# Attention with adapters on one core: a static list scheduler sets the order of all engines

## The chip, the core and the metric

The kernel runs on one core of a Trainium2 chip. The core has a matrix engine (TensorE, PE), three other compute engines (VectorE or DVE, ScalarE or ACT, GpSimd or POOL) and a queue engine (SyncE, SP) that here only issues transfers. Each engine works through its own list of instructions in program order and waits at semaphores for the others; DMA transfers run beside them. The metric is the device time of one execution in microseconds (us).

## The reference

For 8 batches and 8 heads, with 576 positions of 64 values, it computes attention with a relative bias, and sends the result, 4608 rows of 512, through a mixture of 8 low-rank adapters of which each row takes the best two:

```python
scores = (1 / sqrt(64)) * q @ k.T + bias_table[bucket(|i - j|)]   # per head
x = softmax(scores) @ v                                            # then heads side by side
logits = x @ w_gate                                                # (4608, 8)
w = softmax over the two largest logits
out = x + sum over those two e of w[e] * (x @ A[e]) @ B[e]         # A (512,16), B (16,512)
```

The bias depends only on the distance and is constant from distance 128 on, so the kernel multiplies exp(scores) by exp(bias - last bias) in a band around the diagonal, and nowhere else.

## The kernel before

The work goes by pairs of heads: 4 pairs a batch, 32 pairs in all (i). The first 512 positions are the main part; the last 64 of all heads of a batch (the "tails") are loaded and transposed once per batch. For each pair SP loads k, q and v as f32, POOL casts them to bf16 (`cast_kq`, `cast_v`), PE transposes k and q into a PSUM tile kqps (`transposes`), and DVE copies that to kqT. Then come five steps (c = 0 to 4, the last one for the tails): PE makes scores into one of two PSUM tiles sc (`qk`), ACT takes their exp in one instruction of 128x1024 (`softmax_exp`), DVE multiplies the band in place (`band`). PE multiplies the probabilities by v, with a column of ones for the sums, into the only accumulator pv (`pv`, parts 0 to 5); DVE takes the reciprocal rc and writes x (`norm`).

After the fourth pair of a batch its adapters follow, as a list of small pieces (`pieces`): transposes of x (xps to xT), gate logits (lp, lg), the best two by DVE's maximum, df and mk, a small exp on ACT (ex), the gate weights, z (zp to zt), its transpose (zT), and four output tiles (dl to o) that SP stores. Every second batch also sends the tail rows of two batches through. All PSUM tiles but sc and pv share two buffers, "ms".

The order is written out by hand. The main loop goes over i and c; at each step it issues the scores of the next step, the exp of this one, the band of the last one, and the PV parts of the pair before in fixed slots. Loads for pair i + 4, casts for i + 2 and the tail loads of the next batch have slots too, and `BUD` gives each step a budget of adapter pieces, taken from a queue. At the start SP's queue holds k of pair 0 and the tails of batch 0, then the bias chain (the table goes through g_sb, an exp and DRAM, and comes back as the Toeplitz tiles Mr and MHr, from which DVE makes M, MT, MH and MHT), then pairs 1 to 3.

Of the kernel before, what the change touches and what calls it, by code (L numbers as in the profile page):

```python
# [10 lines left out]
FP32 = mybir.dt.float32  # L11
# [16 lines left out]
def kernel(  # L28
# [25 lines left out]
    ctx.enter_context(tc.manual_schedule())  # L54
    cp = ctx.enter_context(tc.tile_pool(name="const", bufs=1))
# [6 lines left out]
    op = ctx.enter_context(tc.tile_pool(name="outs", bufs=4))  # L62
# [16 lines left out]
    def load(i, e0=None, e1=None):
        b, hp = divmod(i, HP)  # L80
        kf = ldp.tile([128, 4, 2, D], FP32, name="kf", tag="kf")
        qf = ldp.tile([128, 2, 256], FP32, name="qf", tag="qf")
        load_nat(kf, k, i, e0 or SY)
        (e1 or SY).dma_start(out=qf, in_=q[b, 2 * hp:2 * hp + 2, 0:S4, :]
                             .rearrange("h (p j) d -> p h (j d)", j=4))
        stg[i] = [kf, qf, None]

    def load_v(i):
        b, hp = divmod(i, HP)
        vf = ldp.tile([128, 4, 2, D], FP32, name="vf", tag="vf")  # L90
        load_nat(vf, v, i, SY)
        stg[i][2] = vf

    def load_tails(b):
        tf = ldp.tile([128, H, D], FP32, name="tf", tag="tf", bufs=2)
        SY.dma_start(out=tf[0:64], in_=k[b, :, S4:, :].rearrange("h p d -> p h d"))
        SY.dma_start(out=tf[64:128], in_=q[b, :, S4:, :].rearrange("h p d -> p h d"))
        tstg[b] = [tf, None]

    def load_vtails(b):  # L100
        vtf = ldp.tile([128, HP, D], FP32, name="vtf", tag="vtf", bufs=2)
        vtr = v[b, :, S4:, :].rearrange("(c e) p d -> e p c d", e=2)
        for e in range(2):
            SY.dma_start(out=vtf[e * 64:(e + 1) * 64], in_=vtr[e])
        tstg[b][1] = vtf
# [28 lines left out]

    def cast_vtail(b, e=None):
        vt = vts[b % 2]
        for h in range(2):
            s = slice(h * 64, (h + 1) * 64)
            copy_on(e or PL, vt[s, :, h * D1:h * D1 + D], tstg[b][1][s])
        tstg.pop(b)  # L140

    load(0, SY, AC)
    load_tails(0)
    btT = cp.tile([H, NB], FP32, tag="btT")
    AC.dma_start(out=btT, in_=bias_table.rearrange("b h -> h b"))
    ident = cp.tile([128, 128], BF16, tag="ident")
    make_identity(nc, ident)

    cast_kq(0, DVE, AC)
    cast_tail(0, DVE)  # L150
    for t in tlTs:
        PL.memset(t, 0.0)
    for t in vts:
        PL.memset(t, 0.0)
        PL.memset(t[0:64, :, D:D1], 1.0)
        PL.memset(t[64:128, :, 2 * D + 1:2 * D1], 1.0)
    for t in vns:
        PL.memset(t[:, :, :, D:D1], 1.0)

    g_sb = cp.tile([H, 512], FP32, tag="g_sb")  # L160
    DVE.memset(g_sb, 0.0)
    bsub = cp.tile([H, NB], FP32, tag="bsub")
    DVE.tensor_scalar(bsub, btT, btT[:, NB - 1:NB], None, op0=ALU.subtract)
    buckets = [_bucket(d, NB) for d in range(256)]
    lo = 0
    runs = []
    for d in range(1, 129):
        if d == 128 or buckets[d] != buckets[lo]:
            runs.append((buckets[lo], lo, d))
            lo = d  # L170
    assert all(x == NB - 1 for x in buckets[128:])
    nsm = 0
    while runs[nsm][0] == nsm and runs[nsm][2] == nsm + 1:
        nsm += 1
    DVE.tensor_copy(g_sb[:, C:C + nsm], bsub[:, :nsm])
    DVE.tensor_copy(
        g_sb[:, C - nsm + 1:C],
        bass.AP(tensor=bsub.tensor, offset=bsub.offset + nsm - 1,
                ap=[bsub.ap[0], [-1, nsm - 1]]))
    for bv, lo, hi in runs[nsm:]:  # L180
        n = hi - lo
        dst = bass.AP(tensor=g_sb.tensor, offset=g_sb.offset + C - hi + 1,
                      ap=[g_sb.ap[0], [hi - 1 + lo, 2], [1, n]])
        DVE.tensor_copy(dst, bsub[:, bv:bv + 1].unsqueeze(2)
                        .to_broadcast((H, 2, n)))
# [11 lines left out]

    def load_bias(h0, h1):
        SY.dma_start(
            out=Mr[:, h0:h1, :],  # L200
            in_=bass.AP(tensor=gt.tensor, offset=gt.offset + h0 * 512,
                        ap=[[1, 128], [512, h1 - h0], [1, MW]]))

    load_bias(0, 2)
    for e in range(2):
        SY.dma_start(
            out=MHr[e * 64:(e + 1) * 64],
            in_=bass.AP(tensor=gt.tensor, offset=gt.offset + e * 512 + 192,
                        ap=[[1, 64], [1024, HP], [1, 192]]))

    def rev(t, o, w, dims):
        return bass.AP(tensor=t.tensor, offset=t[:, o, w:w + 1].offset,
                       ap=[t.ap[0]] + dims)

    def bias_pair(hp, e):
        e.tensor_copy(M[:, 2 * hp:2 * hp + 2],
                      rev(Mr, 2 * hp, 383, [[MW, 2], [-1, 4], [-4, 96]]))

    def bias_tail(e):
        e.tensor_copy(MT, rev(Mr, 0, 127, [[MW, H], [-1, 64]]))  # L220
        e.tensor_copy(MH, rev(MHr, 0, 191, [[192, HP], [-1, 4], [-4, 32]]))
        e.tensor_copy(MHT, rev(MHr, 0, 63, [[192, HP], [0, 2], [-1, 64]]))

    load(1)
    load_v(0)
    load_vtails(0)
    load_bias(2, H)
    load_v(1)
    load(2)
    load_v(2)  # L230
    load(3)
    load_v(3)

# [7 lines left out]

    def load_weights():
        for c in range(4):
            SY.dma_start(out=A_f[:, c], in_=moe_A[:, c * 128:(c + 1) * 128, :]
                         .rearrange("e d r -> d e r"))
        SY.dma_start(out=W_f, in_=moe_w_gate.rearrange("(c p) e -> p c e", p=128))
        SY.dma_start(out=B_f, in_=moe_B.rearrange("e r d -> (e r) d"))

    def cast_weights():
        PL.tensor_copy(Ab, A_f.rearrange("p c e r -> p c (e r)"))  # L250
        PL.tensor_copy(Wb, W_f)
        PL.tensor_copy(Bb, B_f)
        PL.memset(sel, 0.0)
        for e in range(2):
            for hf in range(2):
                s = slice(hf * 64, (hf + 1) * 64)
                PL.tensor_copy(sel[s, e, hf, e * 64:(e + 1) * 64], ident[s, s])


    def tails_T(b):  # L260
        tl = st.pop((b, "tl"))
        ps = msp.tile([128, HP, 2, 64], BF16, name="tps", tag="ms")
        for c in range(HP):
            nc.tensor.transpose(ps[:, c].rearrange("p w s -> p (w s)"),
                                tl[:, 2 * c:2 * c + 2, :], ident)
        t = tlTs[b % 2]
        for e in range(2):
            s = slice(e * 64, (e + 1) * 64)
            DVE.tensor_copy(t[s, :, 0:2, s], ps[s])
        DVE.tensor_copy(t[:, :, 2, :].rearrange("p c (w s) -> p c w s", w=2),  # L270
                        ps[:, :, 1:2, :].to_broadcast((128, HP, 2, 64)))
        tlT[b] = t

    def tails_sc(b):
        t = tlT[b]
        ps = msp.tile([128, HP, 128], FP32, name="ttps", tag="ms")
        for c in range(HP):
            nc.tensor.matmul(ps[:, c, :], lhsT=t[:, c, 0, :], rhs=t[:, c, 2, :],
                             start=(c == 0), stop=True, skip_group_check=True)
# [363 lines left out]
```

## Time and profile before

| | us |
|---|---|
| median of two timed runs | 273.56 (273.54 to 273.57) |
| the profiled execution | 271.94 |
| its span, first to last instruction | 270.1 |
| DVE busy | 210.2 |
| PE busy | 200.9 |
| ACT busy | 163.8 |
| POOL busy | 79.6 |

The mean clock granted to PE was 0.892 of full speed. Busy time is a sum over stages with different limits; what ends a wait is read from the views by stage. PE's matmuls are pipelined and their ends are modelled, so its busy time says more than its use.

### The profile page before, as it was taken

To read this page: it belongs to the slowest core of one execution; us is meant where nothing else is said; L and a number is where in the kernel's file an instruction comes from. 1 tells how busy PE (TensorE), PEld (TensorE's weight loads), DVE (VectorE), ACT (ScalarE), POOL (GpSimd) and SP (SyncE) were. 2 spreads that over 40 slices of the span, in tenths; PEclk is the share of its full clock that TensorE was granted. 3 is DMA by queue.
4 is the path that set the end of the run, shared out by engine and by line. 5 is a ranking of instruction groups with operands and counts; after the bars stand their busy time and mean duration, and the time that the engine had idled before them with its cause. 6 is when DMAs were issued, how large, how long until landed. Compare 5 with 4: busy or idle time off the path is not lost.

```text
span 270.1 us, 7307 instructions
## 1 busy us (share of the span) xinstructions
PE 200.9 (74%) x2872; PEld 139.5 (52%) x2872; DVE 210.2 (78%) x568; ACT 163.8 (61%) x183; POOL 79.6 (29%) x143
## 2 busy tenths in 40 slices
PE   0547918896798698868978598868886897868572
PEld 0224606575566565656556465646564665655540
DVE  1537745887797989896989879898988699869772
ACT  2445843955797568665686477756785677658000
POOL 7035268462211622126312411143315220000000
PEclk9999975997999899986999689988999599979955
DMA  4199998973239922885468803983498503102205
GB/s 117 39 244 238 160 236 224 249 188 79 86 115 242 212 74 93 244 211 139 147 173 198 207 4 113 270 206 97 159 244 204 120 34 137 29 2 77 83 0 194
DMA packets 101082, 39.76 MB, mean 147 GB/s; under 512 B 87088, under 2 KB 96312, under 8 KB 101048
## 3 DMA queue, kind: packets, MB, share of 16 engines
q1 hardware_dynamic: 100512, 39.03, 55.8%
q8 instruction: 22, 0.36, 0.6%
q10 hardware_dynamic: 536, 0.26, 0.4%
q14 instruction: 12, 0.10, 0.1%
HBM read 29.84 MB, written 9.45 MB: 145 GB/s over the span
## 4 chain that ended last, share of the span: by engine, by line
PE 42%; DVE 36%; issue 5%; SPq 5%; ACT 5%; DMA 4%; POOL 1%; ACTq 0%; DVEq 0%; POOLq 0%
PE pv L351 9%; PE sc L306 9%; DVE p L336 7%; DVE x L379 7%; PE kqps L292 5%; ACT p L321 4%; DVE o L491 4%; DVE kqT L295 3%; PE pv L367 3%; SPq L76 3%; PE xps L392 3%; DMA tf<-in_q_dram 3%; DVE rc L378 2%; PE zp L464 2%; PE pv L359 2%
## 5 line engine op out<-in xcount | busy, mean ns | idle before, releaser
L321 ACT ACTIVATE p<-sc 128x1024 bf16<-128x1024 f32 x160 | 155.3, 1023 | 61.3 <-PE sc L306 30.7
L306 PE MATMUL sc<-kqT 64*128 64x512 bf16 x256 | 54.6, 423 | 22.4 <-ACT p L321 19.5
L336 DVE TENSOR_TENSOR p<-p,M 128x512 bf16<-128x512 bf16 (+1 forms) x128 | 65.7, 545 | 1.1 <-ACT p L321 0.2
L351 PEld LDWEIGHTS <-p 128*128 128x128 bf16 x1024 | 44.1, 104 | 24.2 <-issue 12.8
L351 PE MATMUL pv<-vn,p 128*128 128x65 bf16 x1024 | 52.3, 203 | 4.0 <-DVE x L379 2.9
L115 POOL CAST kb<-kf 128x512 bf16<-128x512 f32 x31 | 21.1, 680 | 85.8 <-PE kqps L292 38.2
L306 PEld LDWEIGHTS <-kqT 64*128 64x128 bf16 x256 | 13.5, 94 | 39.0 <-issue 27.8
L295 DVE COPY kqT<-kqps 128x1024 bf16<-128x1024 bf16 x32 | 22.0, 687 | 14.5 <-PE kqps L292 13.8
L379 DVE TENSOR_TENSOR x<-pv,rc 128x640 bf16<-128x640 f32 x32 | 26.4, 824 | 1.1
L115 POOL CAST vn<-vf 128x512 bf16<-128x512 f32 x32 | 20.9, 654 | 16.0 <-PE pv L359 15.1
L491 DVE TENSOR_TENSOR o<-dl,x 128x512 f32<-128x512 f32 x32 | 21.1, 682 | 1.5 <-PE dl L489 1.4
L115 POOL CAST qb<-qf 128x512 bf16<-128x512 f32 x31 | 20.5, 660 | 3.0 <-DMA qf<-in_q_dram 2.3
L489 PE MATMUL dl<-Bb,zT 128*128 128x512 bf16 x32 | 12.2, 409 | 8.2 <-DVE zT L483 4.1
L441 ACT ACTIVATE ex<-df 128x32 f32<-128x32 f32 (+1 forms) x12 | 2.7, 222 | 25.3 <-DVE df L431 25.3
L292 PE MATMUL kqps<-ident,kb 128*128 128x128 bf16 x128 | 14.8, 249 | 3.9 <-POOL kb L115 3.9
L392 PE MATMUL xps<-ident,x 128*128 128x128 bf16 x128 | 11.0, 220 | 8.3 <-DVE x L379 8.3
L378 DVE RECIPROCAL rc<-pv 128x10 f32<-128x10 f32 x32 | 6.9, 217 | 10.8 <-PE pv L367 10.6
L292 PE MATMUL kqps<-ident,qb 128*128 128x128 bf16 x128 | 15.0, 251 | 0.3 <-POOL qb L115 0.2
L115 POOL CAST tl<-tf 128x512 bf16<-128x512 f32 x7 | 4.5, 642 | 36.4 <-DMA tf<-in_q_dram 32.5
L359 PE MATMUL pv<-vn,p 128*128 128x65 bf16 x256 | 14.7, 203 | 0.0
L394 DVE COPY xT<-xps 128x1024 bf16<-128x1024 bf16 x16 | 10.9, 689 | 4.4 <-PE xps L392 4.4
L311 PE MATMUL sc<-tlT,kqT 128*128 128x128 bf16 x128 | 14.4, 243 | 0.0
(81 smaller groups left out, 272.9 us busy)
## 6 DMA issues: line engine op xcount, KB each, us to landing
kf<-in_k_dram SPq DMA_DIRECT2D x64, 128.0 KB, 3.2
vf<-in_v_dram SPq DMA_DIRECT2D x64, 128.0 KB, 3.5
out_dram<-o SPq DMA_DIRECT2D x32, 256.0 KB, 2.6
qf<-in_q_dram SPq DMA_DIRECT2D x31, 256.0 KB, 3.7
tf<-in_k_dram SPq DMA_DIRECT2D x8, 128.0 KB, 3.8
tf<-in_q_dram SPq DMA_DIRECT2D x8, 128.0 KB, 3.4
vtf<-in_v_dram SPq DMA_DIRECT2D x16, 64.0 KB, 2.9
out_dram<-o SPq DMA_DIRECT2D x8, 128.0 KB, 3.0
```

The source lines that it names most:

```text
L115: e.tensor_copy(o, i)
L292: nc.tensor.transpose(ps[:, w, j * 128:(j + 1) * 128], kq[i][w][:, j], ident)
L295: DVE.tensor_copy(t, ps)
L306: nc.tensor.matmul(sc[:, h * 512:(h + 1) * 512], lhsT=t[s, 0, c * 128:(c + 1) * 128], rhs=t[s, 1, :], start=True, stop=True)
L311: nc.tensor.matmul(sc[:, g * 128:(g + 1) * 128], lhsT=t[:, 0, g * 128:(g + 1) * 128], rhs=tt[:, hp, 1, :], start=(g == 0), stop=True, skip ...
L321: AC.activation(p, sc, ACT.Exp, scale=scale)
L336: DVE.tensor_tensor(pm, pm, M[:, 2 * hp:2 * hp + 2, :, x0:x0 + q1 - q0], op=ALU.mult)
L351: nc.tensor.matmul(acc[:, h, s, :], lhsT=p[:, o:o + 128], rhs=vn[:, part, h, :], start=(part == 0 and s == 0), stop=False, skip_group_chec ...
L359: nc.tensor.matmul(acc[:, h, 4, :], lhsT=p[:, g * 128:(g + 1) * 128], rhs=vn[:, g, h, :], start=False, stop=False, skip_group_check=True)
L379: DVE.tensor_tensor(x[:, :, 2 * hp:2 * hp + 2, :].rearrange("p s h d -> p h s d"), acc[:, :, :, :D], rc.unsqueeze(3).to_broadcast((128, 2, ...
L392: nc.tensor.transpose(ps[:, c, t2 * 128:(t2 + 1) * 128], x[:, 2 * half + t2, 2 * c:2 * c + 2, :], ident)
L491: DVE.tensor_tensor(o, ps, xs[b][:, t].rearrange("p h d -> p (h d)"), op=ALU.add)
```

## The change

All hand-written slots go. Each piece of work becomes an operation (`Op`) of one engine with a cost in ns, a latency until others see its result, the operations that it depends on, a due time, and, for tiles of the "ms" and "o" buffers, a place in a ring. Pieces that spanned engines are split: the transposes into two PE groups and a DVE copy, the gate into single DVE instructions and an exp, z into PE groups per 128 rows, the normalisation and the tail band into two instructions each. Some 2500 operations are put in order by a greedy list scheduler while the kernel is built: the engine whose next operation can start first goes next, and among the operations that could start at that moment it takes the one with the smallest due time. The instructions are then issued in that order; on the chip every engine still runs its list in order and waits by semaphores.

Also: the output pool has 6 buffers for 4; the tail transposes of x go to two constant tiles; the clears of tlT move from POOL to DVE; a one-element exp runs first on ACT; the bias table is loaded from SP's queue.

```diff
-    load(0, SY, AC)
-    load_tails(0)
...
-    load_bias(0, 2)
...
-    load(1)
-    load_v(0)
-    load_vtails(0)
-    load_bias(2, H)
-    load_v(1)
...
+    LAT = {"PE": 190, "ACT": 190, "DVE": 110, "PL": 200, "SP": 2600}
+    ops = []
+    rings = {"ms": [2, []], "o": [6, []]}
+
+    def add(eng, cost, fn, deps=(), due=0.0, lat=None, ring=None):
+        o = Op()
...
+    def mm(n):
+        return 16 + n * 0.417 if n <= 130 else 4 + n * 0.417
+
+    def dv(n, fast):
+        return 60 + n / (1.92 if fast else 0.96)
...
+    def load(i, due, ek="SP", eq="SP"):
+        pre = [g_("ck", i - 5), g_("cq", i - 5), g_("cv", i - 5)]
+        a = add(ek, 450, lambda: nat_dma(i, 0, "kf", k, ek), pre[:1], due, 2600)
+        R["lk", i] = add(ek, 450, lambda: nat_dma(i, 1, "kf", k, ek), pre[:1] + [a], due, 2600)
+        R["lq", i] = add(eq, 450, lambda: q_dma(i, eq), pre[1:2], due + .1, 2600)
+        a = add("SP", 450, lambda: nat_dma(i, 0, "vf", v, "SP"), pre[2:], due + 1.0)
+        R["lv", i] = add("SP", 450, lambda: nat_dma(i, 1, "vf", v, "SP"), pre[2:] + [a], due + 1.0)
...
+        d = add("SP", 400, lambda: SY.dma_start(out=g_d.ap(), in_=ge), [e], -20, 2000)
...
+        m0 = add("SP", 400, lambda: mr(0, 2), [d], -20, 2200)
+        h_ = [add("SP", 400, lambda e=e: mhr(e), [d], -19, 2200) for e in range(2)]
+        m1 = add("SP", 400, lambda: mr(2, H), [d], -18, 2600)
...
+            R["tz", i] = add("DVE", 900, lambda t=t: DVE.memset(t, 0.0), (), -25 if i == 0 else 8)
...
+    def mixture(b):
+        due = 20.0 * (b + 1) + 9.5
...
+    load(0, -50, "SP", "ACT")
+    loadt(0, -49)
+    bias_prep()
+    weights()
...
+        t0 = 5.0 * i
+        if i > 0:
+            load(i, t0 - 24 if i > 4 else -22 + i)
+            if hp == 1 and b + 1 < B:
+                loadt(b + 1, t0 - 4)
...
+        a0 = add("PE", 4 * mm(128), lambda i=i: T_pe(i, 0), [R["ck", i], R["id"]], t0 - 4, ring=("ms",))
+        a1 = add("PE", 4 * mm(128), lambda i=i: T_pe(i, 1), [R["cq", i], a0], t0 - 4)
...
+        ev = add("DVE", dv(1024, True), lambda i=i: T_ev(i), [a1, g_("qk", i - 2, 4)], t0 - 3.5)
...
         for c in range(5):
...
+            a = add("PE", 400 if c < 4 else 450, lambda i=i, c=c: qk(i, c),
+                    [ev, R["tl", b], g_("ex", *pv_), g_("qk", *last)], t0 + c - 1.7 - 100)
...
+            x = add("ACT", 925, lambda i=i, c=c: softmax_exp(i, c),
...
+                     g_("ex", *last)], t0 + c - 100)
...
+            if c < 4:
+                n_ = 2 * 4 * (96 if c in (1, 2) else 64)
+                R["bd", i, c] = add("DVE", dv(n_, True), lambda i=i, c=c: band(i, c),
+                                    [x, R["M", hp]], t0 + c + 1.8)
...
+            R["pv", i, p] = add("PE", (10 if p == 5 else 8) * 32.5, lambda i=i, p=p: pv(i, p),
+                                dep + prev, t0 + 5.0 + .5 * p)
...
+        a = add("DVE", 70, lambda i=i: norm1(i), prev, t0 + 8)
...
+    while len(order) < total:
+        best = None
+        for e, cs in cand.items():
+            es = [(t, o) for o in cs if (t := start_of(o)) is not None]
...
+            t0 = min(t for t, _ in es)
+            lim = max(t0, free[e])
...
+            if best is None or t < best[0]:
+                best = (t, o)
...
+    for t, n, o in order:
+        o.fn()
```

## Rows read from the trace of the kernel before

**Rows 1.** The page's first part: busy us (share of the span) xinstructions.

```profile
PE 200.9 (74%) x2872; PEld 139.5 (52%) x2872; DVE 210.2 (78%) x568; ACT 163.8 (61%) x183; POOL 79.6 (29%) x143
```

**Rows 2.** Busy time by stage: stretch, length, engines, clock, DMA share, GB/s.

```profile
0.00:14.27 14.27, 4.26 (x24) 1.97 (x24) 5.18 (x27) 5.77 (x7) 5.20 (x18) 1.00 0.36 86
14.27:50.00 35.73, 23.18 (x256) 14.90 (x257) 19.97 (x45) 18.92 (x21) 19.40 (x34) 0.86 0.96 222
50.00:253.88 203.88, 164.69 (x2521) 117.32 (x2520) 175.95 (x465) 138.64 (x155) 55.04 (x91) 0.92 0.54 143
253.88:270.10 16.22, 8.82 (x71) 5.31 (x71) 9.12 (x34) 0.44 (x2) 0.00 (x0) 0.56 0.25 82
```

**Rows 3.** The same view, one of three like stretches of 10 us.

```profile
160.00:170.00 10.00, 8.92 (x141) 5.96 (x137) 9.92 (x22) 7.78 (x9) 2.04 (x4) 1.00 0.37 110
```

**Rows 4.** Waits from 14.27 to 50 us: waiter, releaser, total us, times, longest.

```profile
DVE tlT L269 <- PE tps L264: 5.6, 1, 5.6
DVE kqT L295 <- PE kqps L292: 4.8, 4, 3.3
...
DVE MT L220 <- DMA Mr<-g_d: 2.7, 1, 2.7
```

**Rows 5.** Timeline of the first 45 us: start, us, engine, line, operation [idle before].

```profile
12.28 1.16 SPq L76 DMA_DIRECT2D kf<-in_k_dram  x2
...
16.40 0.60 SPq L199 DMA_DIRECT2D Mr<-g_d  x1
...
21.87 0.29 DVE L220 COPY MT<-Mr 128x512 bf16<-128x512 bf16 x1 [2.72 <-DMA Mr<-g_d]
...
37.58 0.63 SPq L97 DMA_DIRECT2D tf<-in_q_dram  x1
...
42.49 0.86 DVE L269 COPY tlT<-tps 64x512 bf16<-64x512 bf16 x2 [5.57 <-PE tps L264]
```

**Rows 6.** Waits of DVE from 50 to 253.88 us.

```profile
DVE kqT L295 <- PE kqps L292: 9.0, 12, 2.1
DVE rc L378 <- PE pv L367: 8.4, 12, 1.6
DVE xT L394 <- PE xps L392: 3.8, 7, 0.5
```

**Rows 7.** Waits of ACT and of PE in the same stretch.

```profile
ACT ex L441 <- DVE df L431: 17.7, 10, 2.5
...
PE sc L306 <- ACT p L321: 17.3, 8, 3.5
```

**Rows 8.** Timeline of one stop, 118 to 128 us.

```profile
118.81 0.23 ACT L441 ACTIVATE ex<-df 128x32 f32<-128x32 f32 x1 [2.25 <-DVE df L431]
...
120.01 0.61 PE L306 MATMUL sc<-kqT 64*128 64x512 bf16 x2 [2.05 <-ACT p L321]
...
123.60 0.69 DVE L295 COPY kqT<-kqps 128x1024 bf16<-128x1024 bf16 x1 [1.47 <-PE kqps L292]
...
126.96 0.22 DVE L378 RECIPROCAL rc<-pv 128x10 f32<-128x10 f32 x1 [1.03 <-PE pv L367]
```

**Rows 9.** One microsecond of this stop, columns as in the stages.

```profile
119.00:120.00 1.00, 0.00 (x0) 0.00 (x0) 0.82 (x6) 1.00 (x3) 0.20 (x1) 0.69 0.52 118
```

**Rows 10.** Groups by line: operation, shape, count, busy us, mean ns, idle before.

```profile
L152 POOL MEMSET tlT<- 128x1536 bf16 x2 | 2.7, 1377 | 0.0
```

**Rows 11.** Band multiplies: the groups by form, then minimum/median/maximum of all in ns.

```profile
L336 DVE TENSOR_TENSOR p<-p,M 128x768 bf16<-128x768 bf16 x64 | 40.0, 625 | 0.6 <-ACT p L321 0.2
L336 DVE TENSOR_TENSOR p<-p,M 128x512 bf16<-128x512 bf16 x64 | 29.7, 465 | 0.4
...
L336 DVE TENSOR_TENSOR p<-p,M x128: 409/548/967, 14.3 to 249.6; 128x512 bf16<-128x512 bf16 x64, 128x768 bf16<-128x768 bf16 x64
```

**Rows 12.** Timeline of PE after another stop: first and last score pairs.

```profile
151.38 0.61 PE L306 MATMUL sc<-kqT 64*128 64x512 bf16 x2 [3.52 <-ACT p L321]
...
157.51 0.39 PE L306 MATMUL sc<-kqT 64*128 64x512 bf16 x2
```

More of the change, by code (lines that the diff above doesn't have):

```diff
@@ L88, in load_v @@
[L88 to L105, printed above, removed]
+    class Op:
+        __slots__ = ("eng", "cost", "lat", "fn", "deps", "due", "ring", "end", "done",
+                     "users", "left", "ready", "n")
@@ new lines @@
+    LAT = {"PE": 190, "ACT": 190, "DVE": 110, "PL": 200, "SP": 2600}
[3 more added lines that the diff above has]
+        o = Op()
+        o.eng, o.cost, o.fn, o.due, o.ring = eng, cost, fn, due, ring
+        o.lat = LAT[eng] if lat is None else lat
+        o.deps = [d for d in deps if d is not None]
+        o.end, o.users, o.done, o.ready, o.n = None, [], False, 0.0, len(ops)
+        ops.append(o)
+        return o
@@ L160 @@
+    ident = cp.tile([128, 128], BF16, tag="ident")
+    btT = cp.tile([H, NB], FP32, tag="btT")
     g_sb = cp.tile([H, 512], FP32, tag="g_sb")
-    DVE.memset(g_sb, 0.0)
     bsub = cp.tile([H, NB], FP32, tag="bsub")
[L163 to L185, printed above, removed]
@@ L299, in qk, with T_pe, T_ev @@
+    def T_pe(i, w):
+        if w == 0:
+            st[(i, "kqps")] = msp.tile([128, 2, S4], BF16, name="kqps", tag="ms")
+        ps = st[(i, "kqps")]
+        t = kq.pop((i, w))
+        for j in range(4):
+            PE.transpose(ps[:, w, j * 128:(j + 1) * 128], t[:, j], ident)
+    def T_ev(i):
+        kqT[i] = kqp.tile([128, 2, S4], BF16, name="kqT", tag="kqT")
+        DVE.tensor_copy(kqT[i], st.pop((i, "kqps")))
     def qk(i, c):
@@ new lines, with start_of @@
+    for o in ops:
+        o.left = len(set(map(id, o.deps)))
+        for d in {id(d): d for d in o.deps}.values():
+            d.users.append(o)
+    free = dict.fromkeys(("PE", "ACT", "DVE", "PL", "SP"), 0.0)
+    cand = {e: [] for e in free}
+    for o in ops:
+        if not o.left:
+            cand[o.eng].append(o)
+    order = []
+    total = len(ops)
+    SLACK = 120.0
+    def start_of(o):
+        t = max(o.ready, free[o.eng])
+        if o.ring:
+            n, held = rings[o.ring[0]]
+            if len(held) >= n:
+                rel = held[-n].ring[1]
+                if not rel.done:
+                    return None
+                t = max(t, rel.end)
+        return t
```

843 lines of the change are left out of this document (474 added, 369 removed).

## The prediction

> **What bounds the kernel now.** I read the page's busy line first, then cut the span into stages, then asked in each stage what VectorE (DVE) waits for. DVE is the busiest engine, 210.2 us of the 270.1 us span; TensorE (PE) follows with 200.9 us, but its matmul ends are modelled and overlap, so that share overstates it [rows 1]. I cut at the first band multiply (14.27 us), at 50 us, and at the end of the last normalisation (253.88 us) [rows 2]. From 14.27 to 50 us DVE works 19.97 of 35.73 us, so it idles 15.8 us. From 50 to 253.88 us it works 175.95 of 203.88 us, so it idles 27.9 us, 4.0 us for each of the seven batches in it. The drain after that is one dependent chain of 16.22 us. Three stretches of 10 us show DVE 99% busy with PE at the full clock (one stands in [rows 3]): nothing in the hardware keeps this kernel from running with DVE full. So the question for every edit is how much DVE idling it removes; DVE's own work is the floor.
>
> In the first 50 us the idling has three main causes [rows 4]: 5.6 us for the transposed tails of batch 1, 4.8 us for the transposes of the next pairs, 2.7 us for the bias table. The timeline says why [rows 5]: the tails were only put on SP's queue at 37.58 us, behind loads of four later pairs, and DVE got them at 42.49 us; pair 1's k was queued at 12.28 us, behind the bias chain. After 50 us the waits are 9.0 us on the k/q transposes and 8.4 us on the last PV step [rows 6]. Behind both stands a stop of the in-order queues: ScalarE (ACT) sits 17.7 us at the gate's small exp until DVE has made df, and PE sits 17.3 us at a score matmul until ACT frees a score buffer [rows 7]. One such stop: ACT 2.25 us before 118.81, PE 2.05 us before 120.01; then DVE starves, 1.47 us before the kqT copy at 123.60 and 1.03 us before rc at 126.96 [rows 8]. In that stop the granted clock falls towards half, the 1.2 GHz level (0.69 over the microsecond from 119, in which PE does nothing) [rows 9].
>
> **What the change costs and saves, part by part.** The arithmetic is the same: the same 160 exps, 128 band multiplies and 32 normalisations. Splitting the normalisation, the tail band and the PE groups into single operations adds no instruction. DVE gets two clears of tlT, which took GpSimd 1.38 us each [rows 10], and a one-element clear. The trace has no such clear on DVE; I bound one by 0 and GpSimd's 1.38 us, and take 0 for the path: the first falls in the first 5 us, where DVE waits for k, the second is needed only by batch 1; both uncovered cost 2.8 us, which the upper end of the range has room for. An early exp that loads ACT's table, and the bias load moved from ACT's queue to SP's, go where ACT waited anyway. Six output buffers for four: no DVE wait on an output transfer shows, so 0.
>
> *The head.* The list gives bias steps due -20 and pair 0's casts due -8, so the g_sb copies no longer stand behind the casts. Against that, its cost model makes the second half of each load wait for the first's landing, so first halves of pair 0's v and tails, the bias and part of pair 1 come ahead of k's second half on SP's queue: eighth instead of second. At about 0.5 us an issue [rows 5] that is some 3 us later for k. The first band needs the bias table, which was what it waited for before. I put the first band at 15.0 us (before 14.27), bounds 14.3 and 18.
>
> *14 us to 50 us.* Pairs 1 to 4 are now due -21 to -17 and come ahead of the big bias load, and tails of batch 1 (due 1) right after, so the 5.6 us and most of the 4.8 us go. What is late next is the big bias load (heads 2 to 7). It was issued at 16.40 and MT started at 21.87 us [rows 5]; in the new order some 25 transfers stand before it, at 0.5 to 0.6 us an issue about the same 16 us. Until then DVE has the first pair's four bands, the next kqT copies and tlT, some 4 of 7 us: I keep 3 us of idling, bounds 1 and 8. That drops 12.8 of the 15.8 us.
>
> *From then to the last normalisation.* The scheduler's own costs, summed per pair from the diff with tails and adapters spread over four pairs, are 5.56 us for PE (transposes 0.56, scores 2.05, PV 1.62, the rest 1.33), 5.09 for DVE (bands 1.83, kqT 0.59, normalisation 0.80, the rest 1.87) and 4.79 for ACT (exps 4.62, the rest 0.17). The trace says otherwise: DVE's 195.92 us between 14.27 and 253.88 us [rows 2] is 6.12 us a pair, and a 512-element band is 465 ns [rows 11] against the list's 327. So the order was made for a PE-bound machine and runs on a DVE-bound one. That mostly helps: what DVE consumes is made earlier, relative to DVE, than the list thought, and scores come as far ahead as the three probability buffers let them (due 100 earlier than all else). Idle by cause: the xT waits (3.8 us) and the kqT waits (9.0 us) go, since T of a pair is now due well ahead of its scores; the rc waits (8.4 us) stay, because normalisation, PV and reciprocal are one chain on a single accumulator in either order, and the gate's exp still stands among the large exps in ACT's queue; of the remaining 6.7 us of small gaps I keep half, 3.4. Together 12 us, bounds 3 (as full as [rows 3]) and 28 (nothing gained).
>
> *DVE's work itself.* It is 195.9 us between the cuts. The band multiplies are held up by varying amounts: 409 ns at least, 548 at the median, 967 at most, and 465 ns on average for the small form against its minimum of 409 [rows 11]. That is 56 ns x 64 = 3.6 us; scaled by size, 4.8 us more for the large form. What holds them up is most likely GpSimd, busy 74.4 us in these stages [rows 2]; a fuller DVE meets it more often, so I add 2 us, bounds 0 and 8.4 (twice as much). The Trainium skill's page "SBUF — State Buffer", section "Who interferes with whom", says that a DVE instruction with two SBUF inputs and a GpSimd instruction that reads SBUF block each other for a whole instruction. This speaks against packing DVE tighter beside the same casts, and the spread of 409 to 967 ns agrees with it. By the rule the 2 us belong in the sum; without it the forecast would be 245.6 us.
>
> *The drain.* The same chain, in finer pieces: 16.2 us, bounds 15.5 and 17.
>
> Sum: 15.0 + 195.9 + 2 + 3 + 12 + 16.2 = 244.1 us of span. The profiled execution took 271.94 us for a span of 270.1, so 1.84 lies around it; the median of the two timed runs, 273.56, is 1.62 above the profiled one. 244.1 + 1.84 + 1.62 = 247.6 us.
>
> **The rivals.** *DVE fills up.* Speaking for it: the full stretches [rows 3], and ops on DVE that are 1.2 times what the list thought, so almost everything is ready when its turn comes. Then idling is 3 us and 1 in the head: 14.3 + 195.9 + 0 + 1 + 3 + 15.5 + 3.5 = 233 us; with the middle head terms 238.
>
> *The steady idling stays.* The stop at the gate is a latency around ACT, PE and DVE; a list made with a fast DVE puts the exp too early for the real one, as now. Idling 28, head as forecast: 15 + 195.9 + 2 + 3 + 28 + 16.2 + 3.5 = 263.6 us. With the head gain lost as well (idle 10 instead of 3 there) it is 271 us, within 2% of now; 2% is about what a measurement of this kernel can tell from no change.
>
> *Slower: PE stays at 1.2 GHz.* The order holds PE at score matmuls behind ACT, so it stops often for two us, and the clock falls in such a stop [rows 8, 9]. After the next one, the four score pairs that start from 151.38 to 157.51 us make three steps of 2.04 us, until a pair of these matmuls takes 0.39 instead of 0.61 us again [rows 12]; that is 10.2 us for the five steps of a pair against the 7.5 us of now (239.6 us over 32 pairs). With 6.1 us for a pair in warm stretches, the break-even is a cold share of (7.5 - 6.1)/(10.2 - 6.1) = 34%; the head's gain of 13 us (0.4 us a pair) moves it to 44%. Now the second stage has a mean of 0.92, 16% cold [rows 2]. At 60% cold it is 15 + 32 x (0.6 x 10.2 + 0.4 x 6.1) + 16.2 + 3.5 = 309 us. Against it: matmuls no longer come in blocks behind one wait, and DVE's 99% stretches leave PE at the full clock.
>
> That the change does nothing is excluded: SP's order in the head alone differs.
>
> **How the numbers follow.** Forecast (idling 8 to 18, 241 to 255 us) 0.50; DVE full (below 241) 0.20; steady idling stays (255 to 268) 0.17; head gain lost too (within 2%, 268 to 279) 0.07; PE cold (above 279) 0.06. So faster 0.87, same 0.07, slower 0.06. The range 234 to 263 holds the forecast, some 0.17 of the 0.20 and some 0.13 of the 0.17: 0.80. Likeliest 247.5.
>
> **What the profile of the changed kernel would show.** Right: the tails of batch 1 on SP's queue before 25 us and no DVE wait above 3 us after the big bias load; DVE above 93% busy from 25 us to the last normalisation; exps of pair 2 before the bands of pair 1 are done; the bias load landing near 21 us; a drain of 16 us; the kqT wait nearly gone and the rc wait still in the list. Wrong: DVE's summed work off 198 us by more than 5 (the hold-ups mis-sized); a mean granted clock under 0.85 (the cold rival); SP waiting on an output in front of loads that POOL then waits for; the first band after 18 us; or a drain stretched because adapters of batch 6 are still queued behind the last pair.

## The result, and the profile after

The changed kernel takes 241.06 us (median of two runs, 240.13 and 242.00) against 273.56, a ratio of 0.881 with a 95% interval of 0.867 to 0.896. The forecast was 247.5, the range 234 to 263. The profiled execution took 240.13 us for a span of 238.3, so 1.83 us lie around the span, as before.

The busy line of the page after, which answers to [rows 1]:

```profile
PE 186.4 (78%) x2841; PEld 127.2 (53%) x2872; DVE 204.6 (86%) x571; ACT 164.8 (69%) x184; POOL 78.2 (33%) x141
```

DVE has three instructions more, the two clears of tlT and the one-element clear. Its busy time nevertheless fell by 5.6 us, and the span by 31.8. The same stage cuts as in [rows 2] (first band multiply, 50 us, last normalisation) say where:

```profile
0.00:19.69 19.69, 6.38 (x45) 3.44 (x45) 8.29 (x32) 8.22 (x10) 8.73 (x30) 0.99 0.98 199
19.69:50.00 30.31, 22.56 (x300) 14.85 (x303) 22.68 (x50) 18.95 (x20) 13.85 (x23) 0.78 1.03 212
50.00:223.10 173.10, 150.05 (x2425) 104.68 (x2453) 164.26 (x460) 137.28 (x153) 55.64 (x88) 1.00 0.62 159
223.10:238.30 15.20, 7.41 (x71) 4.20 (x71) 9.35 (x35) 0.39 (x2) 0.00 (x0) 0.75 0.37 127
```

DVE's idle time is each stage's length less its third busy figure. Before the first band it went from 9.1 to 11.4 us; from there to 50 us from 15.8 to 7.6; from 50 us to the last normalisation from 27.9 to 8.8; in the drain from 7.1 to 5.9. Together that is 26.2 us less idling; with the 5.6 us of DVE's own work it makes up the 31.8.

The waits after 50 us, of DVE, ACT and PE (total us, times, longest), answer to [rows 6, 7]:

```profile
DVE rc L316 <- PE pv L311: 1.0, 4, 0.3
...
DVE kqT L241 <- PE kqps L237: 0.7, 2, 0.3
...
DVE xT L340 <- PE xps L334: 0.3, 1, 0.3
...
ACT ex L395 <- DVE df L386: 5.9, 8, 1.5
...
PE pv L296 <- DVE x L324: 5.0, 12, 0.9
...
PE sc L250 <- ACT p L264: 1.2, 4, 0.5
```

All three DVE waits are nearly gone, rc included. ACT's stop at the gate's exp fell from 17.7 to 5.9 us, and PE's stop behind ACT from 17.3 to 1.2. No stop like that of [rows 8, 9] is left: the clock is 1.00 in each of the 17 windows of 10 us from 50 to 220 us, in which DVE works 8.88 to 10.00 us; the best of them answers to [rows 3], and [rows 12] have no counterpart there, as none of the score matmuls of that stage takes over 0.39 us. The other windows are from the head, where the clock reads 0.50, the 1.2 GHz level, twice:

```profile
23.00:25.00 2.00, 1.59 (x16) 0.89 (x14) 2.00 (x7) 1.02 (x1) 0.69 (x1) 0.50 1.26 200
...
31.00:33.00 2.00, 2.00 (x22) 1.28 (x21) 0.61 (x1) 1.20 (x2) 1.70 (x3) 0.50 0.99 249
...
100.00:110.00 10.00, 9.14 (x132) 5.93 (x134) 10.00 (x23) 8.55 (x9) 4.15 (x7) 1.00 0.91 230
```

The head's timeline (start, us, engine, operation, idle before) answers to [rows 5] and, by its waits, to [rows 4]. First the bias chain of the kernel before, then the kernel after:

```profile
6.99 0.11 DVE L163 TENSOR_SCALAR bsub<-btT 8x32 f32<-8x32 f32 x1
...
9.21 0.37 SPq L189 DMA_DIRECT2D g_d<-ge  x1
...
10.55 0.39 SPq L199 DMA_DIRECT2D Mr<-g_d  x1
...
13.60 0.56 DVE L216 COPY M<-Mr 128x768 bf16<-128x768 bf16 x1 [3.28 <-DMA Mr<-g_d]
```

```profile
4.80 0.47 SPq L142 DMA_DIRECT2D kf<-in_k_dram  x1
...
7.07 0.23 DVE L502 TENSOR_SCALAR bsub<-btT 8x32 f32<-8x32 f32 x1 [4.04 <-DMA btT<-in_bias_table_dram]
...
10.15 0.33 SPq L524 DMA_DIRECT2D g_d<-ge  x1
...
14.10 0.37 SPq L527 DMA_DIRECT2D Mr<-g_d  x1
...
17.67 0.56 DVE L539 COPY M<-Mr 128x768 bf16<-128x768 bf16 x1 [2.66 <-DMA Mr<-g_d]
...
19.34 0.43 DVE L545 COPY MH<-MHr 128x512 bf16<-128x512 bf16 x1 [1.11 <-DMA MHr<-g_d]
...
19.69 2.18 DVE L281 TENSOR_TENSOR p<-p,M 128x512 bf16<-128x512 bf16 x3
...
26.49 1.50 SPq L154 DMA_DIRECT2D tf<-in_q_dram  x1
...
30.11 0.61 PE L237 MATMUL kqps<-ident,kb 128*128 128x128 bf16 x4 [3.08 <-POOL kb L133]
```

k's second half is queued at 4.80 us, as forecast, but it isn't what is late. Neither is the bias table's own load: fifth on SP's queue, it lets DVE start at 7.07 us, against 6.99 before. What is late is the rest of that chain. Five loads stand on SP's queue between the write of g and the load that waits for it, and the DMA engines are full (share 0.98 in this stage, 0.36 before): the write is issued 0.94 us later than before, the load 3.55, and the copy of M starts 4.07 us later. Then the list puts the copy of MH, with a wait of 1.11 us for its load, ahead of the first band, which starts at 19.69 instead of 14.27 us. The tails of batch 1 are queued 11 us earlier than in [rows 5]. From the first band to 50 us DVE's largest wait is now this one:

```profile
DVE rc L316 <- PE pv L311: 3.1, 2, 2.5
```

The band multiplies and the clears by form answer to [rows 10, 11]:

```profile
L281 DVE TENSOR_TENSOR p<-p,M 128x768 bf16<-128x768 bf16 x64 | 39.0, 625 | 1.9 <-ACT p L264 1.9
L281 DVE TENSOR_TENSOR p<-p,M 128x512 bf16<-128x512 bf16 x64 | 29.6, 462 | 2.5 <-ACT p L264 2.3
...
L578 DVE MEMSET tlT<- 128x768 uint32 x2 | 1.4, 698 | 0.2
```

A band takes what it took on average, so the fall in busy time isn't from shorter bands. Where then did the 5.6 us go? Two stretches of DVE's timeline, the kernel before and the one after:

```profile
92.09 0.19 DVE L449 TENSOR_REDUCE sm<-mk 128x4 f32<-128x32 f32 x1
92.31 0.18 DVE L450 RECIPROCAL sm<-sm 128x4 f32<-128x4 f32 x1
92.53 0.43 DVE L452 TENSOR_TENSOR gate<-mk,sm 128x32 bf16<-128x32 f32 x1
```

```profile
102.82 0.68 DVE L241 COPY kqT<-kqps 128x1024 bf16<-128x1024 bf16 x1
103.42 0.21 DVE L276 TENSOR_TENSOR p<-p,MH 128x128 bf16<-128x128 bf16 x1
103.55 0.41 DVE L281 TENSOR_TENSOR p<-p,M 128x512 bf16<-128x512 bf16 x1
```

In the first each instruction needs the last one's result and starts 30 to 40 ns after its end. In the second nothing depends on its neighbour, and each starts 80 ns before the end of the one ahead. The sums of the mean durations show it whole: 238.9 us of instructions in 210.2 us of busy time before, 240.9 in 204.6 after. So 28.7 us ran on top of a neighbour before and 36.3 after.

### The profile page after: what moved, and what is told of

Its sections match the earlier page's. It is cut to its first block, busy times and chain, and to the rows that moved or that the text cites. A ratio compares the mean times of both kernels' runs of the same rounds, so it can differ in the third digit from the quotient of the medians.

```text
span 238.3 us, 7332 instructions
## 1 busy us (share of the span) xinstructions
PE 186.4 (78%) x2841; PEld 127.2 (53%) x2872; DVE 204.6 (86%) x571; ACT 164.8 (69%) x184; POOL 78.2 (33%) x141
## 4 chain that ended last, share of the span: by engine, by line
DVE 38%; PE 28%; issue 10%; SPq 8%; DMA 7%; POOL 5%; ACT 1%; another core or an unknown queue 0%; POOLq 0%; DVEq 0%; ACTq 0%
DVE p L281 10%; PE pv L296 8%; DVE x L324 7%; PE sc L250 7%; DMA qf<-in_q_dram 4%; SPq L142 4%; DVE kqT L241 3%; DVE o L456 3%; DVE xT L340 2%; POOL kb L133 2%; SPq L154 2%; PE kqps L237 2%; PE xps L334 2%; PE pv L303 2%; PE dl L452 2%
## 5 line engine op out<-in xcount | busy, mean ns | idle before, releaser
L264 ACT ACTIVATE p<-sc 128x1024 bf16<-128x1024 f32 x160 | 156.9, 1024 | 38.4 <-PE sc L250 29.9
L281 DVE TENSOR_TENSOR p<-p,M 128x512 bf16<-128x512 bf16 (+1 forms) x128 | 67.4, 543 | 4.4 <-ACT p L264 4.2
L296 PE MATMUL pv<-vn,p 128*128 128x65 bf16 x1024 | 51.7, 197 | 12.3 <-DVE x L324 5.9
L296 PEld LDWEIGHTS <-p 128*128 128x128 bf16 x1024 | 41.3, 99 | 28.8 <-issue 7.9
L250 PE MATMUL sc<-kqT 64*128 64x512 bf16 x256 | 52.1, 405 | 3.8 <-DVE kqT L241 1.6
L133 POOL CAST vn<-vf 128x512 bf16<-128x512 f32 x32 | 22.5, 704 | 45.5 <-PE pv L303 32.6
L133 POOL CAST kb<-kf 128x512 bf16<-128x512 f32 x31 | 20.5, 662 | 34.5 <-PE kqps L237 16.2
L237 PE MATMUL kqps<-ident,kb 128*128 128x128 bf16 x128 | 13.3, 230 | 20.1 <-DVE kb L133 9.5
L324 DVE TENSOR_TENSOR x<-pv,rc 128x640 bf16<-128x640 f32 x32 | 26.2, 818 | 0.3
L133 POOL CAST qb<-qf 128x512 bf16<-128x512 f32 x31 | 20.4, 658 | 18.2 <-DMA qf<-in_q_dram 14.3
L237 PEld LDWEIGHTS <-kb 128*128 128x128 bf16 x128 | 8.7, 102 | 23.8 <-DVE kb L133 9.5
L395 ACT ACTIVATE ex<-df 128x32 f32<-128x32 f32 (+1 forms) x12 | 2.6, 223 | 16.2 <-DVE df L386 16.2
L237 PE MATMUL kqps<-ident,qb 128*128 128x128 bf16 x128 | 13.3, 231 | 0.2
L311 PE MATMUL pv<-vt,p 128*128 128x65 bf16 x256 | 13.3, 194 | 0.1
L334 PE MATMUL xps<-ident,x 128*128 128x128 bf16 x128 | 12.3, 219 | 1.4 <-DVE x L324 0.4
L303 PEld LDWEIGHTS <-p 128*128 128x128 bf16 x256 | 10.8, 100 | 4.7 <-issue 4.5
L427 PE MATMUL zp<-Ab,xT 128*128 128x128 bf16 x128 | 11.2, 220 | 2.7 <-DVE kqT L241 2.1
```

Of the source, the lines that this page charges most:

```text
L237: PE.transpose(ps[:, w, j * 128:(j + 1) * 128], t[:, j], ident)
L250: PE.matmul(sc[:, h * 512:(h + 1) * 512], lhsT=t[s, 0, c * 128:(c + 1) * 128], rhs=t[s, 1, :], start=True, stop=True)
L264: AC.activation(p, st.pop((i, c, "sc")), ACT.Exp, scale=scale)
L281: DVE.tensor_tensor(pm, pm, M[:, 2 * hp:2 * hp + 2, :, x0:x0 + q1 - q0], op=ALU.mult)
L296: PE.matmul(acc[:, h, s, :], lhsT=p[:, o:o + 128], rhs=vn[:, part, h, :], start=(part == 0 and s == 0), stop=False, skip_group_check=True)
L303: PE.matmul(acc[:, h, 4, :], lhsT=p[:, g * 128:(g + 1) * 128], rhs=vn[:, g, h, :], start=False, stop=False, skip_group_check=True)
```

## Experiments

None of these kernels leaves out or changes part of the computation; they differ in order, costs and engines. Ratios are against the kernel before, measured beside them on the same chip; its medians there were 271.1 to 273.1 us, its single runs 266.9 to 274.4. The changed kernel was not run again beside them, so differences to it in us are between medians of two series, and the ratios are the safer comparison. The profiled executions of the fourth, sixth and ninth kernel took 234.17, 247.19 and 254.67 us, somewhat above their medians.

**1. The hand order with the gate's exp later.** In the kernel before, the gate's small exp (`m_gate2`) is put two budget slots later, so that more of the large exps stand ahead of it in ACT's order; DVE's half of the gate that uses it (`m_gate3`) moves back with it. Nothing else changes.

```diff
-        l.append((0, lambda: m_gate2(km, 4)))
+        l += [(-1, lambda: None), (-1, lambda: m_gate2(km, 4))]
```

> The kernel before, with one thing moved: the gate's small exp is issued two score steps later, so that two more large exps stand ahead of it on ACT. Theory A (the stop of ACT at the gate's exp, with PE held at a score matmul behind it, makes most of the 27.9 us of DVE idling after 50 us): ACT's wait for df falls from 17.7 us to under 5, PE's wait for ACT from 17.3 to under 5, the clock stays full, and 8 to 14 us go: 260 to 266 us. Theory B (the stop only shows where DVE is late anyway, and the idling comes from the fixed slots): the waits move to another pair of engines and the time stays within 3 us of 273.6.

255.82 us, ratio 0.949 (0.936 to 0.961). The steady stage and its waits:

```profile
50.00:237.02 187.02, 155.60 (x2491) 110.08 (x2518) 175.34 (x464) 138.05 (x154) 57.39 (x91) 0.95 0.59 155
```

```profile
ACT ex L441 <- DVE df L431: 4.7, 4, 1.9
...
DVE rc L378 <- PE pv L367: 0.6, 2, 0.4
```

One line gives 16.3 us of DVE idling back in this stage (27.9 to 11.7 us), and the rc wait, which the prediction had as a chain of its own, falls from 8.4 to 0.6. So the exp that stopped ACT, PE and then DVE held much of the whole gain, 5.1 of 11.9% by the ratios and 17.1 of 31.8 us by the spans of the profiled executions, and no list scheduler was needed for it. The head stays nearly as before: first band at 14.25 us, 14.0 us of idling until 50 us.

**2. No run-ahead of the scores.** The 100 slots by which scores and exps were due ahead of everything are taken off.

```diff
-                    [ev, R["tl", b], g_("ex", *pv_), g_("qk", *last)], t0 + c - 1.7 - 100)
+                    [ev, R["tl", b], g_("ex", *pv_), g_("qk", *last)], t0 + c - 1.7)
...
-                     g_("ex", *last)], t0 + c - 100)
+                     g_("ex", *last)], t0 + c)
```

> The changed kernel with the 100 taken off the due times of scores and large exps, so that they compete with the rest by their own due times. Theory C (the run-ahead of the scores is what keeps ACT, PE and DVE from stopping): DVE's idling between 50 us and the last normalisation goes from 8.8 us back to 16 or more, and the time is 248 us or more. Theory D (the dependences alone let scores run ahead, and the fine pieces do the rest): within 3 us of 241.

237.56 us, 0.880 (0.872 to 0.888): no loss. The steady stage idles 7.1 us against 8.8. Making scores and exps due ahead of everything isn't what fills DVE.

**3. The gate in two blocks.** In the changed kernel the gate's DVE instructions are two operations again, one before and one behind the exp, with the same summed costs.

```diff
-        ms = [add("DVE", 70, lambda t=t: mx(t), [a], due + .01) for t in range(nt)]
-        f = add("DVE", d, df, ms, due + .02)
-        m = add("DVE", d, mk, ms, due + .04)
-        x = add("ACT", 110, ex, [f], due + .03)
...
+        a = add("DVE", 3 * d + 70 * nt, first, pre, due)
+        x = add("ACT", 110, ex, [a], due + .03)
+        return add("DVE", 3 * d + 70, second, [x], due + .05)
```

> The changed kernel with the gate's DVE instructions put back into two blocks, before and after the small exp, as the kernel before has them; nothing else. Theory D (fine pieces matter): DVE's busy time rises by 2 us or more, since dependent instructions in a row cannot overlap, idling rises too, and the time is 245 us or more. Theory C (run-ahead matters, the pieces do not): within 2 us of 241.

247.91 us, 0.918 (0.907 to 0.929), 6.9 us more than the changed kernel by the medians, some 10 by the ratios.

```profile
PE 192.7 (78%) x2841; PEld 132.7 (54%) x2872; DVE 208.8 (84%) x571; ACT 166.0 (67%) x184; POOL 80.8 (33%) x141
```

DVE's 571 instructions sum to 241.5 us by their means, much as in the changed kernel (240.9), but fill 208.8 us against 204.6. Of these 4.2 us, 3.6 are overlap (32.7 us for 36.3) that taking the gate's chain apart had given. The steady stage idles 2.2 us more.

**4. Transfers at their real cost.** The list held 400 to 450 ns for each transfer on SP's queue. Here the costs are closer to what the transfers of the changed kernel's trace occupy at about 200 GB/s.

```diff
-        R["lq", i] = add(eq, 450, lambda: q_dma(i, eq), pre[1:2], due + .1, 2600)
+        R["lq", i] = add(eq, 1200, lambda: q_dma(i, eq), pre[1:2], due + .1, 2600)
...
-        m1 = add("SP", 400, lambda: mr(2, H), [d], -18, 2600)
+        m1 = add("SP", 2700, lambda: mr(2, H), [d], -18, 2600)
...
```

> The changed kernel with the list's transfer costs set to what the DMA engines moved in the first 50 us, about 210 GB/s: 600 ns for a 128 KB load where it had 450, 1200 for q and for an output where it had 450 and 400, 2700 for the big bias load, 1100 for each piece of A. Theory E (the 7.6 us of DVE idling between 19.7 and 50 us come from an order that takes loads for faster than they are): 4 us of it go, 236 to 238 us. Rival (the engines wait on a full DMA in any order): within 2 us of 241.

232.35 us, 0.859 (0.845 to 0.872), 8.7 us less than the changed kernel by the medians, 6.2 by the ratios; the intervals of the two ratios overlap by a little, their runs don't (230.41 to 234.17 against 240.13 to 242.00). The two stages of the head:

```profile
0.00:15.97 15.97, 5.53 (x35) 2.96 (x36) 7.58 (x31) 6.59 (x9) 7.13 (x28) 1.00 0.84 184
15.97:50.00 34.03, 27.82 (x388) 18.43 (x390) 29.67 (x63) 27.62 (x30) 17.30 (x26) 0.95 0.99 202
```

The first band is 3.7 us earlier, and until 50 us DVE does 37.3 us of work instead of 31.0, with no higher DMA share in either stage and less moved per us (184 and 202 GB/s against 199 and 212). So the list had the transfers in a bad order; the DMA engines' rate was not the limit.

**5 and 6. DVE's costs in the list, halved and times 1.2.** The real DVE takes about 1.2 times the list's figure.

```diff
-        return 60 + n / (1.92 if fast else 0.96)
+        return 0.5 * (60 + n / (1.92 if fast else 0.96))
```

> The changed kernel with the list's DVE costs that go by size halved, so that the list thinks DVE has time to spare. Theory F (the order is good because the list puts the gate's exp where a DVE of about the real speed has made df): the stops come back, ACT waits for df 12 us or more after 50 us (5.9 now), DVE's idling there goes from 8.8 to 14 or more, 246 to 252 us. Theory G (any greedy order by dependences does it, the costs hardly matter): within 3 us of 240.

> The changed kernel with the same DVE costs times 1.2, which makes the list's sum per pair 6.1 us as the trace has it. Theory F: ACT's wait for df falls under 4 us, idling after 50 us to 6, 236 to 238 us. Theory G: within 2 us of 240.

Halved: 252.02 us, 0.931 (0.924 to 0.937), 11 us more than the changed kernel by the medians. The steady stage idles 18.2 us, and the wait that grew is PE's on the normalisation:

```profile
PE pv L296 <- DVE x L324: 16.4, 22, 1.3
```

against 5.0 us in the changed kernel; ACT's stop at the exp grows too, from 5.9 to 9.5, and the clock stays at 1.00. The exp's stop grew less than the 12 us expected. The likely reading is that PV steps were put where x would be ready on a DVE twice as fast, and that the one accumulator hands the delay on. Raised by 1.2: 241.71 us, 0.890 (0.884 to 0.896), no gain, though ACT's stop at the exp all but vanishes (1.2 us). The trace is of the execution of 247.19 us, in which DVE waits once for 8.5 us on PV, so it doesn't say how the usual one idles. Costs that are much too low hurt; for the list's own error no harm shows.

**7. The bias chain first.** On top of 4: a second half no longer waits for the first in the list, and the bias table's load, the write of g and the first Toeplitz load are due first.

```diff
-                (), -30.0)
+                (), -60.0)
...
-        d = add("SP", 400, lambda: SY.dma_start(out=g_d.ap(), in_=ge), [e], -20, 2000)
+        d = add("SP", 400, lambda: SY.dma_start(out=g_d.ap(), in_=ge), [e], -45, 2000)
```

> The transfer costs of e4, and two more edits of the head: the second half of a load no longer depends on the first in the list, and the bias table is loaded first, with its way through DRAM due before the loads of pair 1. Theory H (DVE's first band waits for the bias chain, which waits behind loads): pair 0's k lands some 3 us earlier, the first band starts at 12 to 13 us for 15.97 in e4, 228 to 230 us. Rival (the transfers are full from the start, so what comes earlier for one makes another late): the first band is earlier but DVE's idling to 50 us grows by as much, within 1.5 us of e4.

229.49 us, 0.848 (0.842 to 0.854). The first band starts at 14.27 us, later than the 12 to 13 expected, and DVE idles 12.3 us until 50 us, against 19.0 in the changed kernel and 24.9 before.

**8. All of it.** Kernel 7 with no run-ahead and DVE's costs times 1.2.

> e7 with the 100 off the due times of scores and exps (e2) and DVE costs times 1.2 (e6). If the parts add up: 2 to 4 us below e7, 225 to 227 us. If they do not, it is within 1.5 us of e7.

226.16 us, 0.834 (0.830 to 0.839). The steady stage idles 3.7 us.

**9. The hand order with three edits.** Kernel 1, with pair 1's loads and batch 0's v ahead of the bias chain and the tails of batch 1 loaded before pair 3.

```diff
     load_tails(0)
+    load(1)
+    load_v(0)
+    load_vtails(0)
...
+    load_tails(1)
+    load_vtails(1)
```

> The kernel before with its hand-written slots, the gate's exp two steps later (e1), pair 1's loads and batch 0's v ahead of the bias chain on SP, and batch 1's tails ahead of pair 3's loads. Theory I (the two places that the trace shows make the gain, whoever orders them): the 5.6 us wait for the tails and the 3 us wait of the first kqT go as well, 246 to 250 us, and the rest to 240 is DVE's finer interleaving. Rival (SP's and the DMA engines' time is short in the head, so one wait is traded for another): within 2 us of e1's 255.8.

252.21 us, 0.926 (0.917 to 0.936), 3.6 us less than kernel 1 and a smaller gain than hoped for. The first band comes later, at 16.03 instead of 14.25 us. The timeline behind it:

```profile
20.24 0.63 SPq L97 DMA_DIRECT2D tf<-in_q_dram  x1
...
33.29 0.62 POOL L252 CAST Ab<-A_f 128x512 bf16<-128x512 f32 x1 [4.29 <-DMA A_f<-in_moe_A_dram]
...
38.04 0.61 POOL L115 CAST tl<-tf 128x512 bf16<-128x512 f32 x1
...
39.42 0.86 DVE L271 COPY tlT<-tps 64x512 bf16<-64x512 bf16 x2 [6.46 <-PE tps L266]
```

The tails are on SP's queue at 20.24 us and still reach DVE at 39.42. POOL works in order: its cast of the adapter matrix A waits 4.29 us for A's load, the other weight casts and two later casts follow, and only then the tails. The late queueing in [rows 5] was one cause of two.

**12. The weight casts behind the tails.** Kernel 9 with those weight casts one pair later.

```diff
-                    if i == 1:
+                    if i == 2:
                         cast_weights()
```

> The hand order of the run before with one more edit: GpSimd's casts of the adapter weights (A, gate, B, and the selection tile) move one pair later, behind the cast of batch 1's tails. Nothing is left out. Theory L (the tails wait because GpSimd works in order and its weight casts wait for A): the 6.5 us wait of VectorE's tlT copy falls under 1.5 us, the idle time from the first band to 50 us falls from 10.5 to 5 to 7 us, and the time is 246 to 248 us against 252.2. Rival M (the first 50 us are bound by the DMA engines, which are full, so another wait, for k and q of later pairs or for the big bias load, takes its place): the tlT wait goes, but the idle time before 50 us stays above 9 us and the time is within 2 us of 252.2.

```profile
32.45 0.93 POOL L115 CAST tl<-tf 128x512 bf16<-128x512 f32 x1
...
33.95 0.86 DVE L271 COPY tlT<-tps 64x512 bf16<-64x512 bf16 x2 [0.28 <-PE tps L266]
```

The wait falls from 6.46 to 0.28 us, and DVE's idling from the first band to 50 us from 10.5 to 4.8. The median is 246.57 us, 0.917 (0.902 to 0.932); one of its runs took 252.67, and the interval overlaps that of kernel 9, so the trace shows the mechanism and the time agrees without proving it.

**10 and 11. Work off DVE, or off GpSimd.** Both start from kernel 8. In 10, ACT copies kqT for the odd pairs. In 11, ACT makes the 32 casts of v that GpSimd made; DVE's instructions are the same.

```diff
-        ev = add("DVE", dv(1024, True), lambda i=i: T_ev(i), [a1, g_("qk", i - 2, 4)], t0 - 3.5)
+        ev = add("ACT" if i % 2 else "DVE", 1020 if i % 2 else dv(1024, True), lambda i=i: T_ev(i),
...
-        R["cv", i] = add("PL", 650, lambda i=i: cv_(i, "PL"),
+        R["cv", i] = add("ACT", 620, lambda i=i: cv_(i, "ACT"),
```

> e8 with the copy of kqT on ACT for every second pair: 16 copies of 0.68 us less on DVE (10.9 us), 16 of about 1.02 us more on ACT (16 us). Theory J (DVE's own work is the floor, ACT has room at 164 of 224 us): 8 to 10 us of it show, 216 to 218 us. Rival (ACT's queue order now delays the scores that wait for these copies, and PE or ACT sets the end): 223 us or more.

> e8 with the 32 casts of v on ACT in place of GpSimd: 20 us less on GpSimd, 20 us more on ACT, DVE's instructions unchanged. Theory K (GpSimd's casts hold up DVE's band multiplies): the mean band of 512 elements falls from 493 to about 470 ns and of 768 from 604 to about 585, all DVE work falls by 3 to 5 us, 221 to 224 us if ACT's queue bears it. Rival (the bands vary for another reason): means unchanged within 5 ns and DVE work unchanged.

Kernel 10: 229.40 us, 0.846 (0.840 to 0.853), slower than kernel 8 with 6.3 us less DVE work: the steady stage idles 10.8 us instead of 3.7, and in 3.4 us of it DVE waits for results of ACT. Kernel 11: 222.52 us, 0.813 (0.804 to 0.822), the fastest. Some of DVE's groups by form in 8, then in 11:

```profile
L281 DVE TENSOR_TENSOR p<-p,M 128x768 bf16<-128x768 bf16 x64 | 38.1, 604 | 0.5 <-ACT p L264 0.4
L281 DVE TENSOR_TENSOR p<-p,M 128x512 bf16<-128x512 bf16 x64 | 31.5, 493 | 0.0
...
L241 DVE COPY kqT<-kqps 128x1024 bf16<-128x1024 bf16 x32 | 21.7, 680 | 4.3 <-PE kqps L237 4.2
```

```profile
L281 DVE TENSOR_TENSOR p<-p,M 128x768 bf16<-128x768 bf16 x64 | 37.5, 595 | 0.8 <-ACT p L264 0.7
L281 DVE TENSOR_TENSOR p<-p,M 128x512 bf16<-128x512 bf16 x64 | 29.1, 455 | 0.2
...
L241 DVE COPY kqT<-kqps 128x1024 bf16<-128x1024 bf16 x32 | 21.8, 682 | 3.7 <-PE kqps L237 3.5
```

The busy lines of 8 and of 11:

```profile
PE 184.1 (82%) x2842; PEld 129.3 (58%) x2872; DVE 202.3 (90%) x571; ACT 163.0 (73%) x184; POOL 79.6 (36%) x141
```

```profile
PE 180.9 (83%) x2842; PEld 126.4 (58%) x2872; DVE 195.6 (90%) x571; ACT 177.5 (81%) x216; POOL 57.9 (27%) x109
```

ACT takes over 14.5 us of work, GpSimd loses 21.7 (79.6 to 57.9), and DVE's unchanged instructions take 6.7 us less (202.3 to 195.6). By the sum of mean durations (239.8 to 233.6) 6.2 us of that is shorter instructions, and they are mostly those with two inputs from SBUF, like the bands; the kqT copy from PSUM stays (680 and 682 ns).

Means alone don't show that the casts were the cause, since the order moved too: in kernel 2, with every cast on GpSimd, the small band has a mean of 457 ns, in the changed kernel 462. The single records of kernel 8's trace do show it. Of its 64 small bands, the 33 that meet no GpSimd instruction take 410 ns on average, the 31 that meet one 581, up to 869; its kqT copies take 680 and 679. In the kernel before, such bands take 415 (48 of them) and 613 (16). Counted so over bands and tail bands, the hold-ups come to 13.7 us in kernel 8 and 8.4 in kernel 11. So GpSimd's instructions hold up such DVE instructions, by an amount that also hangs on the order: with all casts on GpSimd it is 9.9 us in the kernel before and up to 16.2 in the others (kernel 4). The Trainium skill's page "SBUF — State Buffer", section "Who interferes with whom", has such a lock between DVE and GpSimd; these runs agree with it.

## Why the prediction was right, and where not

The direction and the main mechanism held: a hand order whose in-order queues stop each other, on a chip that can keep DVE full. That the sum came only 5.8 us too high is in part luck, since errors of both signs cancel: head +4.7, DVE's work -11.0, idling before 50 us +4.6, after it -3.2, drain -1.0. Two of the prediction's own signs of being wrong came up, a first band after 18 us and DVE's work more than 5 us off 198. Of its signs of being right, the kqT wait and the drain held; q's half of batch 1's tails was queued at 26.49 us instead of before 25, and DVE was 92.2% busy from 25 us on instead of above 93.

- *The head, 15.0 us with bounds 14.3 and 18: wrong.* 19.69 us. The step that failed is "eighth instead of second, some 3 us later for k; the first band needs the bias table, which was what it waited for before". It priced k's delay and took the bias chain as unchanged. But the chain's write and loads now stood among early loads of later pairs, on SP's queue and on the DMA engines, and lost 3.55 us up to the issue of Mr's load alone. Kernels 4 and 7 show it: with transfers costed by size that load is issued at 11.91 us and the first band starts at 15.97, with the chain first at 9.48 and 14.27.
- *3 us of idling until 50 us, bounds 1 and 8: mis-sized, 7.6 us.* The tails and the big bias load were no longer late (waits of 0.8 and 0.9 us, none over 2.5), so that reasoning stood. DVE's longest waits were now on PV (3.1 us) and on the exps (2.4). Behind them PE waited 4.6 us for casts, 3.08 of it at 30.11 us, where POOL had itself waited 2.70 us for a load of q. What PE's slow pace in this stage cost is not shown: pairs of score matmuls take 0.61 us there until 35.23 us and 0.39 from 37.1, and kernel 3, which idles 8.8 us in the same stage, has the same slow pairs until 35.60.
- *12 us of steady idling, bounds 3 and 28: near, 8.8 us; its working was half right.* The kqT and xT waits went. The rc waits, said to stay (8.4 us), went to 1.0. The step "normalisation, PV and reciprocal are one chain in either order" failed: kernel 1 shows that the rc wait was the far end of the stop at the gate's exp. "The gate's exp still stands among the large exps" was right for a third (5.9 of 17.7 us), and kernel 5 shows how a list with a much too fast DVE brings the idling back, though there more at the normalisation (16.4 us) than at the exp (9.5). The rival "the steady idling stays" built on such a list, and did not come about with one whose DVE was 1.2 times too fast.
- *DVE's work, 195.9 + 2: wrong, 186.9 between the cuts.* 3.1 us of it merely moved ahead of the first band. The rest is the overlap of neighbours that don't depend on each other, which the prediction had not thought of ("splitting adds no instruction" was right, and not all). The 2 us for hold-ups were about right: of the 128 bands 54 instead of 42 meet a GpSimd instruction, and counted as in experiment 11 the hold-ups of bands and tail bands grow from 9.9 to 12.5 us. The busy time hides them, since other instructions got a little shorter and more of them overlap.
- *"DVE's own work is the floor": too simple.* Kernel 10 has less of it and is slower, because DVE then waits more, about half of that for ACT.
- *The drain, 16.2: right, 15.2.* The tlT clears at no cost: right; both run from 1.53 us, where DVE waits for its inputs.
- *The slower rival, PE at 1.2 GHz: its mechanism shows only in the head.* After 50 us the granted clock is 1.00 and no score matmul takes over 0.39 us, where 24 of them took over 0.5 before.

Not settled: why costs times 1.2, which nearly end ACT's stop at the exp, gain nothing alone; and how the overlap gained beyond the gate's 3.6 of 7.6 us divides. Part of it seems to come from fewer stops alone, as kernel 1, still in the hand order, has 31.1 us of overlap for 28.7. Nor were the small changes (six output buffers, constant tiles for the tail transposes, the early exp) tried by themselves.

## What to carry to other kernels

Before rewriting an order, look for the one small instruction that stands too early in an in-order queue: here its stop on ACT showed up as waits of PE and then of DVE on other lines, and moving it alone gave 5.1 of the 11.9%. In this list scheduler, transfer costs by size and the order of the first loads were worth more than run-ahead or compute costs raised by a fifth. Give the engine that bounds the kernel independent neighbours, and ask which other engine's work makes its instructions longer.

## What was unexpected of the hardware

- Neighbouring DVE instructions overlap by about 80 ns when independent and stand 30 to 40 ns apart when dependent; with 571 instructions the sum of the overlaps went from 28.7 to 36.3 us, and blocking the gate alone took 3.6 of it back (kernel 3).
- A DVE multiply with two SBUF inputs is held up when it meets a GpSimd instruction: in kernel 8 a small band takes 410 ns alone and 581 beside one, while a copy from PSUM takes 680 and 679.
- Early in a kernel the granted clock of a row need not be PE's pace. In kernel 3 it reads 1.00 while a pair of score matmuls takes 0.61 us, the time it takes in the changed kernel at a reading of 0.50:

```profile
31.00:33.00 2.00, 2.00 (x17) 1.10 (x16) 1.51 (x4) 1.02 (x1) 1.65 (x3) 1.00 1.01 240
...
31.02 0.61 PE L250 MATMUL sc<-kqT 64*128 64x512 bf16 x2
```

In the first stage too the clock reads 1.00 before and 0.99 after, while a score matmul takes 0.60 us at 10.4 and at 11.5 us, and 0.39 later on. There the durations of the matmuls tell PE's pace.
